# Raw keys and values summed by three adds on GpSimd and one reduction on VectorE, with the ranks' matmuls a tile later

## The chip, the cores and the metric

One core of a Trainium2 chip runs the whole program. The metric is the device time of one execution in microseconds. The kernel before took 1160.65 us, the median of three runs (1155.35 to 1163.43).

## What is computed

Eight batches of eight heads with 576 queries of 64 numbers go through an attention whose keys and values are first averaged over eight neighbours, so that 72 pooled keys per head are left. The 4608 rows of 512 numbers that result go through two mixtures of eight experts, one after the other; each row is sent to the expert with its largest gate logit.

```python
def _attn_ref(q, k, v):
    k_p = k.reshape(B, H, Sp, pool, D).mean(axis=3)
    v_p = v.reshape(B, H, Sp, pool, D).mean(axis=3)
    scores = scale * np.matmul(q, k_p.transpose(0, 1, 3, 2))
    scores = scores - np.max(scores, axis=-1, keepdims=True)
    attn = np.exp(scores)
    attn = attn / (np.sum(attn, axis=-1, keepdims=True) + 1e-09)
    return np.matmul(attn, v_p).astype(np.float32)

def _moe_ref(x, w_gate, w_output_gate, w1, w2):
    logits = x @ w_gate
    e_idx = np.argmax(logits, axis=1)
    ...
    for e in range(E):
        mask = e_idx == e
        h = np.maximum(x[mask] @ w1[e], 0.0)
        ye = h @ w2[e]
        out[mask] = gate_w[mask, None] * eom[mask, e, None] * ye
```

The second mixture has the same form, with a bias by modality in its logits and without the output gate.

## The kernel before

The program has two parts: an attention stage, and then the two layers of experts. The change edits the first.

**Tiles.** The 4608 queries are worked off in 36 tiles of 128 (`NT`), four and a half tiles to a batch. The loop at L639 runs over the tiles as a pipeline that is written out by hand: in turn i, TensorE computes the scores of tile i (L364), multiplies the transposed exponentials of tile i-2 with the values (L401) and transposes the exponentials of tile i-1 (L385). VectorE takes the maxima of tile i (L369) and normalises tile i-2 (L415 to L422). ScalarE takes the exponentials of tile i (L376) and evicts the transposes (L392). The order on each engine is the order of the code, and each engine takes its instructions in that order.

**Sums of raw keys and values.** Per batch, the eight planes of raw keys (and likewise of values) come in two loads of four planes into two tiles of a ring of seven (`ring`, L488). `pool_sum` (L298) adds them up: `half` adds planes 2 and 3 to planes 0 and 1 of one tile (L301, 576 elements per partition, on GpSimd), twice per sum; `both` on VectorE adds the two tiles (L305, 576 elements), gives the second tile back to the ring and adds the two planes that are left (L307, 288 elements); `spread` (L319 on ScalarE) copies the heads apart into KB, which the scores read, or VT, from which TensorE makes the values' operand VB (L332, L334). There are 16 such sums; the first keys are summed in another way (L526 to L531), and of the first values one half is added on VectorE, so that 15 sums have L305 and L307. The halves are handed out by `gp_work` at the end of a turn (two per turn, with scatters between them), and `both` and `spread` come three turns after the last half (`DELAY`), or earlier where a tile needs them.

**Routing.** The tiles form groups of four (`groups`, L347; two groups of two at the end). When a group's last tile is normalised, `route` (L427) puts a list of small operations for the whole group into `fill`: the choice of the expert (L451 to L458; L457 writes the one-hot of the choice in bf16), the ranks of the rows within their expert (`ranks`, L442: five small matmuls on TensorE, L445 and L447, that read that one-hot), the gate's factors (L460 to L463, L467, L469, L471, L472), the rows' places (L464 to L470), and last the hand-over of the group's scatters (L480, indirect DMAs on GpSimd) to the queue `gpq`. `filler` takes one entry at a time from the head of this list, about eight per turn, between VectorE's other work (two at a time while more than 16 are left). An entry with the letter "p" is TensorE's: `filler` at other places stops before it, and `filler(9, "p")` at the end of a turn, behind the transposes, takes it.

After the fourth group twelve more operations choose the favourite expert (L128 to L139), whose weights are then loaded in the attention stage and split into a high and a low part, one tile of weights per turn: the high part on ScalarE (L613, L616), the low one on GpSimd (L617).

**Layers.** Each expert's rows come back in blocks of 256; TensorE multiplies with three products of high and low parts (L757 and L799). The blocks' tiles xH and xL and the activations HH and HL lie in the pool `wp` behind the weights W1H and W1L (L100 to L107).

Of the kernel before, what the change touches and what calls it, by code (L numbers as in the profile page):

```python
# [10 lines left out]
F32R = mybir.dt.float32r  # L11
# [3 lines left out]
ALU = mybir.AluOpType  # L15
# [7 lines left out]
P = 128  # L23
# [10 lines left out]
NF = F // P  # L34
# [13 lines left out]
def kernel(ctx, tc, q, k, v, wg, wo, w1, w2, mod, wg2, bias2, v1, v2, out):  # L48
# [51 lines left out]
    W1H = [wp.tile([P, F], F32R, name=f"W1H{i}") for i in range(ND)]  # L100
    W1L = [wp.tile([P, F], F32R, name=f"W1L{i}") for i in range(ND)]
    W2H, W2L = [], []
    xH = wp.tile([P, ND, BLK], F32R, name="xH")
    xL = wp.tile([P, ND, BLK], F32R, name="xL")
    xg0 = wp.tile([P, 2, XW], F32, name="xg0")
    HH = [wp.tile([P, 2, BLK], F32R, name=f"hh{i}") for i in range(NF // 2)]
    HL = [wp.tile([P, 2, BLK], F32R, name=f"hl{i}") for i in range(NF // 2)]  # L107
    dummy = cst.tile([P, XW], F32, name="dummy")
    GP.memset(dummy, 0.0)
    GP.memset(dummy[:, DM + 1:DM + 2], float(N))  # L110
# [187 lines left out]
    def pool_sum(eng, first, raw, dst, scale):  # L298
        def half(lo, eng):
            r = raw[lo]  # L300
            eng.tensor_tensor(r[:, 0:2], r[:, 0:2], r[:, 2:4], op=ALU.add)  # L301

        def both():

            DVE.tensor_tensor(raw[0][:, 0:2], raw[0][:, 0:2], raw[4][:, 0:2], op=ALU.add)  # L305
            ring.append(raw[4])
            DVE.tensor_tensor(raw[0][:, 2], raw[0][:, 0], raw[0][:, 1], op=ALU.add)  # L307

        def spread():
            apart_heads(dst, raw[0][:, 2], slice(0, NG), scale)  # L310
            ring.append(raw[0])

        return [lambda: half(0, first), lambda: half(4, eng)], [both, spread]
# [34 lines left out]
    where = {T: (g, i) for g, ts in enumerate(groups) for i, T in enumerate(ts)}  # L348
    st, lgs, xgs, fill = {}, {}, {}, []

    def filler(n=1, kinds="v"):
        n += len(fill) > 16
        while n and fill and fill[0][0] in kinds:
            fill.pop(0)[1]()
            n -= 1
# [71 lines left out]
    def route(g):  # L427
        G = len(groups[g])
        T0 = groups[g][0]
        lg = lgs[g][:, 0:G, 0:E]  # L430
        og = lgs[g][:, 0:G, E:2 * E]
        bc = lambda t: t.unsqueeze(2).to_broadcast([P, G, E])
        c8 = lambda t: t.unsqueeze(1).to_broadcast([P, G, E])
        t5 = lambda n, dt=F32, bufs=2: sm.tile([P, 5], dt, name=n, bufs=bufs)[:, 0:G]
        t58 = lambda n, dt=F32: sm.tile([P, 5, E], dt, name=n)[:, 0:G]
        m, km, z, ez, df, ssum = (t5(n) for n in ("rm", "rkm", "rz", "rez", "rdf", "rss"))
        di = t5("rdi", I32, 3)
        a, oh, d, a2, ex, dd = (t58(n) for n in ("ra", "roh", "rd", "ra2", "rex", "rdd"))
        ohb = t58("rohb", BF16)
        pr = []  # L440

        def ranks():  # L442
            p = ranks_in[0]()
            pr.append(p)
            PE.matmul(p[:, 0:G], lhsT=tri_b, rhs=ohb, start=True, stop=False, skip_group_check=True)  # L445
            for dl in range(1, G + 1):
                PE.matmul(p[:, dl:G + 1], lhsT=ones_b, rhs=ohb[:, 0:G + 1 - dl], start=False, stop=dl == G, skip_group_check=True)  # L447

        V = lambda f: ("v", f)
        fill.extend([  # L450
            V(lambda: DVE.tensor_reduce(m, lg, axis=AX.X, op=ALU.max)),  # L451
            V(lambda: DVE.tensor_tensor(a, lg, bc(m), op=ALU.is_ge)),
            V(lambda: DVE.tensor_tensor(d, lg, bc(m), op=ALU.subtract)),
            V(lambda: DVE.tensor_tensor(a, a, c8(rev), op=ALU.mult)),
            V(lambda: ACT.activation(ex, d, AF.Exp)),
            V(lambda: DVE.tensor_reduce(km, a, axis=AX.X, op=ALU.max)),
            V(lambda: DVE.tensor_tensor(ohb, c8(rev), bc(km), op=ALU.is_equal)),  # L457
            V(lambda: DVE.tensor_tensor(oh, c8(rev), bc(km), op=ALU.is_equal)),  # L458
            ("p", ranks),
            V(lambda: DVE.tensor_tensor(a2, oh, og, op=ALU.mult)),  # L460
            V(lambda: DVE.tensor_reduce(ssum, ex, axis=AX.X, op=ALU.add)),
            V(lambda: DVE.tensor_reduce(z, a2, axis=AX.X, op=ALU.add)),
            V(lambda: ACT.activation(ez, z, AF.Exp, scale=-1.0)),  # L463
            V(lambda: DVE.tensor_tensor(dd, pr[0][:, 0:G], c8(base1), op=ALU.add)),  # L464
            V(lambda: DVE.tensor_tensor(base1, base1, pr[0][:, G], op=ALU.add)),
            V(lambda: DVE.tensor_tensor(dd, dd, oh, op=ALU.mult)),
            V(lambda: DVE.tensor_scalar(ssum, ssum, 1e-9, None, op0=ALU.add)),  # L467
            V(lambda: DVE.tensor_reduce(df, dd, axis=AX.X, op=ALU.add)),
            V(lambda: DVE.tensor_scalar(ez, ez, 1.0, None, op0=ALU.add)),  # L469
            V(lambda: DVE.tensor_copy(di, df)),  # L470
            V(lambda: DVE.tensor_tensor(ssum, ssum, ez, op=ALU.mult)),  # L471
            V(lambda: DVE.reciprocal(xgs[g][:, 0:G, DM], ssum)),  # L472
            V(lambda: gpq.extend((lambda i=i: scatter1(di, i, xgs[g])) for i in range(G))),
        ])
        if g == 3:
            fill.extend(V(f) for f in fav1)
            fill.append(V(lambda: sjobs.append(first_weights)))
# [159 lines left out]
            sjobs.append(load)  # L637

    for i in range(NT + 1):  # L639
        if 0 < i - 2 < NT:  # L640
            stage_et_evict(i - 2)
        if vbs:
            vbs.pop()()
        second = []
        if splits and (splits[0][0] <= i or i >= NT):
            first, *second = splits.pop(0)[1]
            first()
        if 0 < i < NT:
            for a in range(i == 2, 2):
                scores(i, a)  # L650
        if i == NT:
            t = turned(ps_a, ("ps0", "ps1"))
            turn(t, xg0, (0,))
        if 0 <= i - 2 < NT:
            stage_av(i - 2)
        if 0 < i < NT:
            for a in range(2):
                if i == 1:
                    v0.pop(0)()
                maxima(i, a)  # L660
                stage_exp(i, a)
        if i == 2:
            prefetch(2)
            load_q(2)
            flush(ldq, 2)
        if lasts and i >= summed.get(lasts[0][0], i) + DELAY:
            lasts.pop(0)[1]()
        filler()
        if 0 <= i - 2 < NT:
            normalise(i - 2)  # L670
        if 0 <= i - 1 < NT:
            stage_et(i - 1)
        if i == NT:
            stage_et_evict(i - 1)
            turn(t, xg0, (1,))
            high(t, xH)
            low(t, xH, xL)
            stage_av(i - 1)
            normalise(i - 1)
        else:  # L680
            filler(9, "p")
        filler()
        for _ in range(1 + i % 2):
            if ldq:
                ldq.pop(0)[1]()
        gp_work(2)
        if fetched == B - 1 and len(ring) == KV and not W2H and not ldq:
            kctx.close()
            w2p = ctx.enter_context(tc.tile_pool(name="w2p", bufs=1, side="right", reuse_waits="tile"))
            W2H += [w2p.tile([P, 2, DM], F32R, name=f"W2H{i}") for i in range(NF // 2)]  # L690
            W2L += [w2p.tile([P, 2, DM], F32R, name=f"W2L{i}") for i in range(NF // 2)]
        for f in second:
            f()
        if sjobs and len(splits) < 3 and (W2H or not late2[0]):
            f = sjobs.pop(0)()
            if isinstance(f, tuple):
                splits.append((i + 3, f))
        if i == 0:
            flush(sums, 1)
        if i == 1:  # L700
            v0.pop()()
            DVE.memset(KB[1], 0.0)
            DVE.memset(VT[1], 0.0)
            scores(2, 0)
            stage_et_evict(0)
            evicts = [prep_v(0, 0), prep_v(0, 1, "pm")]
            for f in evicts:
                f()
        if late:
            vbs.append(prep_v(*late.pop(0)))  # L710
        if i + 1 < NT:
            prepare(cols(i + 1)[-1][0], True)
        if i + 2 < NT:
            b = cols(i + 2)[-1][0]
            if b > prepped:
                prepare(b)
                prepped = b
                if 2 < b + 2 < B:
                    prefetch(b + 2)
        if i < NT and cols(i)[-1][0] > fetched - 2 and fetched + 1 < B:  # L720
            fetched += 1
            load_q(fetched)
        tags = {e[0] for e in sums}
        for tag in {e[0] for e in lasts} - tags - set(summed):
            summed[tag] = i
# [439 lines left out]
```

## Time and profile before

| | us |
|---|---|
| median of three runs | 1160.65 |
| the profiled execution | 1161.28 |
| its span, first to last instruction | 1159.6 |
| PE busy (share of the span) | 1081.8 (93%) |
| DVE busy | 661.0 (57%) |
| ACT busy | 395.0 (34%) |
| POOL busy | 271.0 (23%) |
| mean granted clock of TensorE | 0.973 |

All times in the rows further down are microseconds from the start of the span unless marked ns. PE is TensorE, DVE VectorE, ACT ScalarE, POOL GpSimd; L12 is line 12 of the kernel before. A busy PE counts matmuls that are pipelined, so its busy time is no measure of its peak; where it is idle, the bracket behind a row says for how long and what it waited for.

### The profile page before, as it was taken

The page shows a single profiled execution, that of the slowest core. Times are in us where ns is not written, and L with a number is a line of the kernel's source. Part 1 is how long each engine was busy: PE and PEld are TensorE (multiplying, and loading weights), DVE is VectorE, ACT ScalarE, POOL GpSimd, SP SyncE. Part 2 cuts the span into 40 slices and gives each one's busy share as a digit, 9 for nine tenths or more (in the row PEclk, how much of TensorE's full clock was granted, in tenths as well). Part 3 has the DMA queues.
Part 4 walks back from the last instruction along what each step waited for, and adds up shares of the span by engine and source line. Part 5 has one row for each costly group of instructions (what it writes and reads, how often), then busy time and mean ns, then how long its engine had stood idle before and what let it go on. Part 6 is the DMA issues. An engine that isn't in the chain of part 4 may idle for free. (4 is left out here: it accounts for less than half of the span.)

```text
span 1159.6 us, 21927 instructions
## 1 busy us (share of the span) xinstructions
PE 1081.8 (93%) x7058; PEld 970.4 (84%) x7058; DVE 661.0 (57%) x2154; ACT 395.0 (34%) x924; POOL 271.0 (23%) x249
## 2 busy tenths in 40 slices
PE   7988888999997999799999998999999999999993
PEld 6878787988876898688889977899889889988983
DVE  6988887777989877877987676111211221111110
ACT  6766674123634323314512232221212332211120
POOL 7545355100614400411610003100011040001000
PEclk8989998999999999899999998999999999999997
DMA  9766543641735511512450001721111111111000
GB/s 345 271 217 216 191 138 146 218 141 46 265 107 185 185 41 45 173 51 84 144 203 31 20 21 60 282 84 39 38 47 56 38 44 52 38 39 48 29 20 21
DMA packets 52090, 128.12 MB, mean 110 GB/s; under 512 B 6957, under 2 KB 10029, under 8 KB 51760
## 3 DMA queue, kind: packets, MB, share of 16 engines
q1 hardware_dynamic: 42928, 97.28, 25.5%
q0 software_dynamic: 8960, 28.47, 6.3%
q8 instruction: 88, 1.44, 0.5%
q14 instruction: 114, 0.93, 0.2%
HBM read 92.51 MB, written 34.27 MB: 109 GB/s over the span
## 5 line engine op out<-in xcount | busy, mean ns | idle before, releaser
L747 DVE SCALAR_TENSOR_TENSOR hl<-h,hh 128x512 fp32r<-128x512 f32 x140 | 94.9, 690 | 357.1 <-ACT hh L746 355.8
L799 PE MATMUL y<-W2H,hh 128*128 128x512 f32 x608 | 238.5, 403 | 11.4 <-DVEq L1024 8.0
L799 PE MATMUL y<-W2L,hh 128*128 128x512 f32 x608 | 238.2, 401 | 0.0
L799 PE MATMUL y<-W2H,hl 128*128 128x512 f32 x608 | 236.3, 400 | 1.2 <-DVE hl L747 1.1
L823 DVE CUSTOM_DVE_ANT_0 junk<-y,wg2b 128x512 f32<-128x512 f32 x312 | 192.9, 686 | 2.8 <-ACTq L1026 2.1
L746 ACT ACTIVATE hh<-h 128x512 fp32r<-128x512 f32 x140 | 83.4, 597 | 313.7 <-PE h L757 310.2
L802 ACT ACTIVATE y<-y,xg 128x512 f32<-128x512 f32 x76 | 52.3, 689 | 316.8 <-PE y L799 269.2
L799 PEld LDWEIGHTS y<-W2H,hh 128*128 128x128 f32 x608 | 115.6, 191 | 39.2 <-issue 7.1
L799 PEld LDWEIGHTS y<-W2H,hl 128*128 128x128 f32 x608 | 115.9, 191 | 31.1 <-DVE hl L747 3.5
L799 PEld LDWEIGHTS y<-W2L,hh 128*128 128x128 f32 x608 | 116.1, 191 | 25.8
L1046 POOL DMA_INDIRECT out_dram<-y,ti x37 | 36.4, 983 | 382.2 <-ACT y L802 259.0
L757 PE MATMUL h<-xH,W1L 128*128 128x256 f32 x608 | 123.5, 285 | 0.2 <-DVE W1L L193 0.2
L757 PE MATMUL h<-xH,W1H 128*128 128x256 f32 x608 | 99.9, 287 | 7.8 <-issue 3.8
L811 POOL TENSOR_TENSOR W2L<-R,W2H 128x1024 fp32r<-128x1024 f32 x32 | 76.9, 2435 | 121.3 <-ACT W2H L1028 101.7
L877 POOL DMA_INDIRECT xs<-y,qdi x39 | 38.5, 987 | 273.8 <-DVE lg L823 246.9
L757 PE MATMUL h<-x2H,W1L 128*128 128x256 f32 x512 | 102.2, 280 | 0.2 <-DVE W1L L193 0.2
L757 PE MATMUL h<-xL,W1H 128*128 128x256 f32 x608 | 98.2, 284 | 0.0
L757 PEld LDWEIGHTS h<-xH,W1L 128*128 128x128 f32 x608 | 95.5, 193 | 0.4 <-DVE W1L L193 0.4
L757 PEld LDWEIGHTS h<-xH,W1H 128*128 128x128 f32 x608 | 84.0, 193 | 8.4 <-issue 7.2
L757 PE MATMUL h<-x2H,W1H 128*128 128x256 f32 x512 | 82.7, 283 | 3.7 <-DVE qdd L867 3.3
L757 PEld LDWEIGHTS h<-xL,W1H 128*128 128x128 f32 x608 | 84.4, 193 | 0.0
L401 PE MATMUL pav<-VB,et 96*128 96x162 f32 (+1 forms) x480 | 72.8, 318 | 12.2 <-DVE ll L420 5.7
(245 smaller groups left out, 1646.5 us busy)
## 6 DMA issues: line engine op xcount, KB each, us to landing
R<-in_w_dram SPq DMA_DIRECT2D x56, 512.0 KB, 5.2
xg<-xs SPq DMA_DIRECT2D x72, 258.0 KB, 2.7
kv<-in_v_dram SPq DMA_DIRECT2D x16, 576.0 KB, 6.4
R<-in_v_dram SPq DMA_DIRECT2D x16, 512.0 KB, 7.5
kv<-in_k_dram SPq DMA_DIRECT2D x14, 576.0 KB, 5.2
qt<-in_q_dram SPq DMA_DIRECT2D x14, 576.0 KB, 9.5
xs<-dummy SPq DMA_DIRECT2D x18, 258.0 KB, 2.6
wraw<-in_w_dram SPq DMA_DIRECT2D x8, 512.0 KB, 3.9
```

Of the source, the lines that this page charges most:

```text
L401: PE.matmul(v4[r0:r0 + n, a, j:j + 2, :], lhsT=st[T]["et"][a][:, j, r0:r0 + n], rhs=VB[b % 3][:, a * 3 + j, :], start=j == 0, stop=j == 2, ...
L746: ACT.activation(HH[kk], p, AF.Relu)
L747: DVE.scalar_tensor_tensor(HL[kk], in0=p, scalar=0.0, in1=HH[kk].bitcast(F32), op0=ALU.max, op1=ALU.subtract)
L757: PE.matmul(p[:, c2, :], lhsT=W[d][:, c:c + P], rhs=x[:, d, :], start=n == 0, stop=n == 3 * ND - 1)
L799: PE.matmul(p, lhsT=X[f // 2][:, f % 2, hf * P:(hf + 1) * P], rhs=W[f // 2][:, f % 2, :], start=i == 0, stop=i == 3 * NF - 1)
L802: ACT.activation(S["y"][:, hf, 0:DM], p, AF.Copy, scale=S["xg"][:, hf, DM:DM + 1])
L811: GP.tensor_tensor(W2L[j], R2[j], W2H[j].bitcast(F32), op=ALU.subtract)
L823: DVE.tensor_tensor_reduce(out=M["junk"][:, e % 2], in0=p, in1=M["wg2b"][:, e, :], scale=1.0, scalar=0.0, op0=ALU.mult, op1=ALU.add, accum ...
L877: apart("xs2", GP.indirect_dma_start(xs2, IDX(ap=di[:, hf:hf + 1], axis=0), y[:, hf, :], None, bounds_check=E * REG - 1, oob_is_err=False))
L1046: apart("out", GP.indirect_dma_start(out, IDX(ap=S["ti"][:, hf:hf + 1], axis=0), S["y"][:, hf, 0:DM], None, bounds_check=N - 1, oob_is_err ...
```

## The change

`pool_sum` puts more of a sum on GpSimd. `half` writes its result into the first tile at once: the first half into planes 0 and 1, the second into planes 2 and 3 of the same tile. After the second half the second tile goes back to the ring, and a third add on the same engine adds planes 2 and 3 to planes 0 and 1. VectorE then sums the two planes that are left by one `tensor_reduce`, which reads them through a view with the plane innermost. For the first values, where VectorE does the second half, it does the third add too.

`route` marks the turn in which the one-hot is issued, and `filler(9, "p")` does nothing in that turn, so the ranks' matmuls are issued at the end of the next one at the earliest. The list is put into another order: the sum of the exponentials, its 1e-9 and the gate's exponential stand ahead of the ranks, and behind them stand nine entries instead of fourteen.

HH and HL are allocated right behind W1H and W1L, ahead of xH, xL and xg0.

```diff
     W2H, W2L = [], []
+    HH = [wp.tile([P, 2, BLK], F32R, name=f"hh{i}") for i in range(NF // 2)]
+    HL = [wp.tile([P, 2, BLK], F32R, name=f"hl{i}") for i in range(NF // 2)]
     xH = wp.tile([P, ND, BLK], F32R, name="xH")
     xL = wp.tile([P, ND, BLK], F32R, name="xL")
     xg0 = wp.tile([P, 2, XW], F32, name="xg0")
-    HH = [wp.tile([P, 2, BLK], F32R, name=f"hh{i}") for i in range(NF // 2)]
-    HL = [wp.tile([P, 2, BLK], F32R, name=f"hl{i}") for i in range(NF // 2)]
...
         def half(lo, eng):
             r = raw[lo]
-            eng.tensor_tensor(r[:, 0:2], r[:, 0:2], r[:, 2:4], op=ALU.add)
+            eng.tensor_tensor(raw[0][:, lo // 2:lo // 2 + 2], r[:, 0:2], r[:, 2:4], op=ALU.add)
+            if lo:
+                ring.append(r)
+                eng.tensor_tensor(raw[0][:, 0:2], raw[0][:, 0:2], raw[0][:, 2:4], op=ALU.add)
 
         def both():
 
-            DVE.tensor_tensor(raw[0][:, 0:2], raw[0][:, 0:2], raw[4][:, 0:2], op=ALU.add)
-            ring.append(raw[4])
-            DVE.tensor_tensor(raw[0][:, 2], raw[0][:, 0], raw[0][:, 1], op=ALU.add)
+            DVE.tensor_reduce(raw[0][:, 2], raw[0][:, 0:2].rearrange("p j c -> p c j"), axis=AX.X, op=ALU.add)
...
+    now, marked = [0], [0]
+
+    def mark():
+        marked[0] = now[0]
+
     def filler(n=1, kinds="v"):
+
+        if kinds == "p" and marked[0] == now[0]:
+            return
         n += len(fill) > 16
...
-            V(lambda: DVE.tensor_tensor(ohb, c8(rev), bc(km), op=ALU.is_equal)),
+            V(lambda: (mark(), DVE.tensor_tensor(ohb, c8(rev), bc(km), op=ALU.is_equal))),
             V(lambda: DVE.tensor_tensor(oh, c8(rev), bc(km), op=ALU.is_equal)),
-            ("p", ranks),
             V(lambda: DVE.tensor_tensor(a2, oh, og, op=ALU.mult)),
             V(lambda: DVE.tensor_reduce(ssum, ex, axis=AX.X, op=ALU.add)),
             V(lambda: DVE.tensor_reduce(z, a2, axis=AX.X, op=ALU.add)),
+            V(lambda: DVE.tensor_scalar(ssum, ssum, 1e-9, None, op0=ALU.add)),
             V(lambda: ACT.activation(ez, z, AF.Exp, scale=-1.0)),
+            ("p", ranks),
+            V(lambda: DVE.tensor_scalar(ez, ez, 1.0, None, op0=ALU.add)),
             V(lambda: DVE.tensor_tensor(dd, pr[0][:, 0:G], c8(base1), op=ALU.add)),
             V(lambda: DVE.tensor_tensor(base1, base1, pr[0][:, G], op=ALU.add)),
             V(lambda: DVE.tensor_tensor(dd, dd, oh, op=ALU.mult)),
-            V(lambda: DVE.tensor_scalar(ssum, ssum, 1e-9, None, op0=ALU.add)),
+            V(lambda: DVE.tensor_tensor(ssum, ssum, ez, op=ALU.mult)),
             V(lambda: DVE.tensor_reduce(df, dd, axis=AX.X, op=ALU.add)),
-            V(lambda: DVE.tensor_scalar(ez, ez, 1.0, None, op0=ALU.add)),
             V(lambda: DVE.tensor_copy(di, df)),
-            V(lambda: DVE.tensor_tensor(ssum, ssum, ez, op=ALU.mult)),
             V(lambda: DVE.reciprocal(xgs[g][:, 0:G, DM], ssum)),
...
     for i in range(NT + 1):
+        now[0] = i
```

Where the instructions stand, first on TensorE around the first group's ranks, in the kernel before: `ps` are scores, `pav` the values' products, `pe` the transposes, `rohb` the one-hot, `pm` the ranks.

```order
L385 MATMUL pe_660<-ident,ee 96x128 x3
L445 LDWEIGHTS tri_b
L445 MATMUL pm<-rohb,tri_b 128x32
L447 LDWEIGHTS ones_b
L447 MATMUL pm<-rohb,ones_b 128x32
...
L364 MATMUL ps_679<-KB_182,qt 128x144 x2
L364 MATMUL ps_682<-KB_182,qt 128x144 x2
L401 MATMUL pav<-VB_185,et_674 128x162 x3
```

And in the changed kernel, whose lines are some nine further down (L373 is the scores' line, L410 the values', L394 the transposes', L454 and L456 the ranks'):

```order
L394 MATMUL pe_665<-ident,ee 96x128 x3
L373 MATMUL ps_679<-KB_182,qt 128x144 x2
L373 MATMUL ps_682<-KB_182,qt 128x144 x2
L410 MATMUL pav<-VB_185,et_674 128x162 x3
L410 MATMUL pav<-VB_185,et_676 128x162 x3
L394 MATMUL pe_713<-ident,ee 96x128 x3
...
L454 LDWEIGHTS tri_b
L454 MATMUL pm<-rohb,tri_b 128x32
L456 LDWEIGHTS ones_b
L456 MATMUL pm<-rohb,ones_b 128x32
```

The ranks of a group have moved behind the next tile's scores, values' products and transposes.

Second, on GpSimd from one group's copy into its tile `x` to the next one's, in the kernel before: `kv` are tiles of the ring, `xs` takes the scatters.

```order
L411 COPY x<-meta 128x4x3
L301 TENSOR_TENSOR kv_196<-kv_196 128x576
L301 TENSOR_TENSOR kv_194<-kv_194 128x576
L480 DMA xs_66<-x,rdi 37888x516 x2
L301 TENSOR_TENSOR kv_198<-kv_198 128x576
L480 DMA xs_66<-x,rdi 37888x516
L301 TENSOR_TENSOR kv_197<-kv_197 128x576
L480 DMA xs_66<-x,rdi 37888x516
```

And in the changed kernel (L420 the copy, L301 a half, L304 the third add, L489 a scatter):

```order
L420 COPY x<-meta 128x4x3
L489 DMA xs_66<-x,rdi 37888x516 x2
L301 TENSOR_TENSOR kv_195<-kv_195 128x576
L301 TENSOR_TENSOR kv_195<-kv_197 128x576
L304 TENSOR_TENSOR kv_195<-kv_195 128x576
L301 TENSOR_TENSOR kv_194<-kv_194 128x576
L489 DMA xs_66<-x,rdi 37888x516
L301 TENSOR_TENSOR kv_194<-kv_199 128x576
L304 TENSOR_TENSOR kv_194<-kv_194 128x576
L489 DMA xs_66<-x,rdi 37888x516
```

Two of a group's four scatters have moved behind the next copy, and each sum has a third add right behind its second half.

Third, on VectorE the first tile's normalisation and the sum of the second batch's keys, in the kernel before:

```order
L305 TENSOR_TENSOR kv_198<-kv_198,kv_199 128x576
L307 TENSOR_TENSOR kv_198<-kv_198 128x288
L415 TENSOR_SCALAR rs<-pav 128x8
L417 RECIPROCAL rs<-rs 128x8
L419 TENSOR_TENSOR x<-pav,rs 128x512
L420 TENSOR_TENSOR ll<-pav,rs 128x128
L422 TENSOR_REDUCE lgs<-ll 128x16
```

And in the changed kernel (L424 to L431 the normalisation, L308 the reduction):

```order
L424 TENSOR_SCALAR rs<-pav 128x8
L426 RECIPROCAL rs<-rs 128x8
L428 TENSOR_TENSOR x<-pav,rs 128x512
L429 TENSOR_TENSOR ll<-pav,rs 128x128
L431 TENSOR_REDUCE lgs<-ll 128x16
L308 TENSOR_REDUCE kv_198<-kv_198 128x288
```

The sum has moved behind the normalisation.

## Rows read from the trace of the kernel before

**Rows 1.** Windows by stage: length, busy us of each engine, PEclk, DMA share, GB/s.

```profile
22.43:183.64 161.21, 134.33 (x1039) 125.58 (x1037) 139.49 (x404) 112.85 (x395) 83.29 (x69) 0.95 0.59 207
183.64:195.87 12.23, 11.27 (x69) 10.77 (x67) 7.74 (x34) 4.70 (x16) 1.73 (x2) 0.77 0.49 186
195.87:1159.60 963.73, 919.75 (x5842) 819.06 (x5841) 501.38 (x1694) 264.85 (x471) 167.95 (x124) 0.98 0.26 88
```

**Rows 2.** Waits of PE, 20 to 197 us: total us, times, longest us.

```profile
PE pm L445 <- DVE rohb L457: 14.6, 6, 4.5
PE pav L401 <- DVE ll L420: 5.7, 3, 3.3
```

**Rows 3.** Timeline of PE, DVE and POOL, 55 to 70 us: start, length, instruction, idle before.

```profile
56.38 0.82 PE L385 MATMUL pe<-ident,ee 128*96 128x128 f32 x6
59.75 0.19 PE L445 MATMUL pm<-rohb,tri_b 128*128 128x32 bf16 x1 [2.56 <-DVE rohb L457]
61.57 1.78 PE L364 MATMUL ps<-KB,qt 128*128 128x144 f32 x8
65.50 1.15 PE L364 MATMUL ps<-KB,qt 128*128 128x144 f32 x8
...
56.70 3.00 DVE L457 TENSOR_TENSOR rohb<-rev,rkm 128x32 bf16<-128x32 f32 x1
...
56.89 2.75 POOL L301 TENSOR_TENSOR kv<-kv 128x576 f32<-128x576 f32 x2
```

**Rows 4.** Six lines, 0 to 197 us: xcount, ns min/median/max, first and last start.

```profile
L457 DVE TENSOR_TENSOR rohb<-rev,rkm x9: 174/193/5429, 40.7 to 196.7; 128x32 bf16<-128x32 f32 x8, 128x16 bf16<-128x16 f32 x1
...
L305 DVE TENSOR_TENSOR kv<-kv,kv x15: 747/750/2896, 13.9 to 143.6; 128x576 f32<-128x576 f32 x15
...
L307 DVE TENSOR_TENSOR kv<-kv x15: 458/459/1872, 14.7 to 146.5; 128x288 f32<-128x288 f32 x15
...
L422 DVE TENSOR_REDUCE lgs<-ll x35: 354/368/376, 23.8 to 194.2; 128x16 f32<-128x128 f32 x35
...
L369 DVE TENSOR_REDUCE nm<-ps x72: 440/448/459, 8.4 to 185.9; 128x4 f32<-128x288 f32 x72
...
L301 POOL TENSOR_TENSOR kv<-kv x29: 1393/1408/1558, 11.2 to 135.0; 128x576 f32<-128x576 f32 x29
```

**Rows 5.** Timeline of DVE and POOL, 68 to 82 us.

```profile
68.77 0.13 DVE L472 RECIPROCAL x<-rss 128x4 f32<-128x4 f32 x1
77.61 3.01 DVE L457 TENSOR_TENSOR rohb<-rev,rkm 128x32 bf16<-128x32 f32 x1
...
69.69 1.01 POOL L480 DMA_INDIRECT xs<-x,rdi  x1 [10.05 <-DVE x L472]
77.81 2.75 POOL L301 TENSOR_TENSOR kv<-kv 128x576 f32<-128x576 f32 x2
```

**Rows 6.** Timeline of DVE and PE, 114 to 185 us.

```profile
114.66 2.90 DVE L136 CAST fei<-fef 128x2 int32<-128x2 f32 x1
...
178.02 5.43 DVE L457 TENSOR_TENSOR rohb<-rev,rkm 128x32 bf16<-128x32 f32 x1
...
120.29 3.02 PE L401 MATMUL pav<-VB,et 96*128 96x162 f32 x12 [3.31 <-DVE ll L420]
...
162.23 0.18 PE L445 MATMUL pm<-rohb,tri_b 128*128 128x32 bf16 x1 [1.85 <-DVE rohb L457]
...
183.50 0.18 PE L445 MATMUL pm<-rohb,tri_b 128*128 128x32 bf16 x1 [4.46 <-DVE rohb L457]
```

**Rows 7.** Timeline of ACT and PE, 20 to 26 us.

```profile
22.59 0.90 ACT L319 ACTIVATE KB<-kv 64x288 f32<-64x288 f32 x2 [0.36 <-DVE kv L307]
...
24.05 1.92 PE L401 MATMUL pav<-VB,et 96*128 96x162 f32 x12 [0.47 <-ACT et L392]
```

**Rows 8.** The page's costliest groups: first layer, the two x tiles.

```profile
L757 PE MATMUL h<-xH,W1L 128*128 128x256 f32 x608 | 123.5, 285 | 0.2 <-DVE W1L L193 0.2
L757 PE MATMUL h<-x2H,W1L 128*128 128x256 f32 x512 | 102.2, 280 | 0.2 <-DVE W1L L193 0.2
```

## The prediction

> **What bounds the kernel now.** I read the stretches first. From 195.87 us on, the two expert layers run with TensorE busy 919.8 of 963.7 us, and the change touches no instruction there. What it edits is in front: 33 starts of a tile's scores lie between 22.43 and 183.64 us, 161.2 us for 32 tiles, 5.04 us each, of which TensorE works 134.3 us at a granted clock of 0.95 [rows 1]. So the attention stage is where time can go, and a microsecond less there is a microsecond off the end, since the layers wait for the last tile.
>
> Next came the waits of TensorE in that stage. The largest is on the change's path: six times, 14.6 us in all, the ranks' matmuls (L445) wait for VectorE's one-hot (L457), and three times, 5.7 us, the values' matmuls (L401) wait for VectorE to empty their PSUM tile (L420) [rows 2]. TensorE takes its queue in order, so a wait of the ranks holds all behind it.
>
> Then I asked why VectorE is late, in the order of time around one such wait. The one-hot is an operation of 32 elements, and here it lasts 3.00 us: it starts at 56.70, GpSimd's two adds of raw values run from 56.89 to 59.64, and it ends just after them. TensorE is idle for 2.56 us, and the eight scores' matmuls behind it then take 1.78 us, where those of the next tile take 1.15 [rows 3]. The same operations elsewhere show the rule of this trace: the one-hot takes 0.174 to 5.429 us, the add of two SBUF planes (L305) 0.747 to 2.896, the next (L307) 0.458 to 1.872, while the reductions L422 and L369, one input each, stay within 0.354 to 0.376 and 0.440 to 0.459. GpSimd's add is hardly disturbed, 1.393 to 1.558 [rows 4]. So two-input work on VectorE pays for GpSimd's adds, and a request made just ahead of a run pays for the whole run.
>
> Last, why they meet in every group of four tiles. The scatters of a group wait on GpSimd for the group's last factor (L472, 68.77). The first starts at 69.69, and the queue that stood behind it is then worked off, down to two adds at 77.81 to 80.56, exactly when the next group's one-hot comes, at 77.61 (3.01 us) [rows 5].
>
> **The change part by part.**
>
> The sums. Per sum VectorE drops L305 and L307, 0.75 + 0.46 = 1.21 us undisturbed, and gets one reduction of 576 reads. No row shows that one; the contiguous reduction L369 gives 0.448 x 576/288 = 0.90 us, the strided L422 gives 0.368 x 576/128 = 1.66 us (fixed cost multiplied too). I take the middle, 1.28, because it steps between two planes for each result but writes few. Undisturbed VectorE gains nothing; it gains where the two adds were disturbed. It lies beside TensorE's work, so I book 0 by itself. GpSimd gets a third add of 1.41 us in 14 sums (the first values' stands on VectorE), 20 us, in a queue that mostly waits. The reduction now waits for the third add; behind it on VectorE stand a tile's maxima or its normalisation, for which ScalarE and then TensorE wait, and its cover is the distance of three tiles at which the code puts it (without that, 1.41 us per sum, the third rival).
>
> The order. The ranks now stand a tile later on TensorE, behind the next tile's scores, values and transposes, so the one-hot has a tile (5 us) to come. Nothing else is held: nobody reads the ranks before the fill list reaches them, and the list stops there for a tile. That stop is the second effect: the last factor comes at the end of its tile, the scatters are handed over a tile later, and on GpSimd the next keys' three adds stand behind two scatters. By the durations of rows 4 and 5, with the last factor at t: one scatter to t+1.3, two adds to t+4.1, three scatters to about t+8, three adds to t+12.3. The next group's selection (L452 to L458) falls at t+4 to t+6, beside scatters, and the three adds fall in the tile in which the list stands still. So the waits go, and do not only move.
>
> Gains: of the 14.6 us, 4.46 and 1.85 stand behind splits of weights on GpSimd [rows 6], which stay; the other four, 14.6 - 6.3 = 8.3, I count whole. Of the 6.3 I count half, 3.1: VectorE will be as late, but TensorE has a tile's work before it notices. The 5.7 us come with the choice of the favourite expert and an add: a cast of two numbers took 2.90 there, and the values' matmuls then waited 3.31 [rows 6]. One run of two adds still meets that list: half, 2.9. The clock: 134.3 x 0.05 = 6.7 us of TensorE's work is lost to the low level of 1.2 GHz, which the rows show behind such waits (3.02 us for twelve values' matmuls at 120.29 [rows 6], 1.92 for the twelve at 24.05 [rows 7]); half, 3.4. Together 17.7.
>
> Costs: the second batch's keys are now reduced behind tile 0's normalisation, so the copies into KB at 22.59, for which the evictions and then the values' matmuls at 24.05 wait [rows 7], come up to 2.3 us later; the next value sum, which met an add there, gives most of it back: 0.5, between 0 and 2.3. In the first group GpSimd has nine adds in a row, and the selection meets them: by the 3.00 us for two adds, three cost 4.4, less 1.6 paid there now: 2.8, between 0 and 4.4. By the Trainium skill (SBUF — State Buffer, Who interferes with whom) the loser is blocked until the first one's instruction ends, so a third add would cost nothing more and this term would be 0; rows 3 show a wait through two adds, so I keep the row's price. The first ranks of the layer get their one-hot some 0.4 us later, as four more operations stand ahead of it: 0.4, between 0 and 0.8.
>
> The activations' place: the same bytes at other addresses. The nearest rows are the two x tiles at different places, 285 and 280 ns per matmul [rows 8]; if 5 ns hung on the place, the 3 x 608 matmuls that read HH and HL would give or take 9 us. I take 0: the slower one also runs the first block, at the low clock.
>
> Sum: 17.7 - 0.5 - 2.8 - 0.4 = 14.0. The profiled execution took 1161.28 us, so 1147.3; it stands 0.6 above the median of the runs shown, so 1146.7, said as 1147.
>
> **The rivals.** First, the waits move: VectorE stays as late, and the values' matmuls wait in place of the ranks. For it: at 178.02 the one-hot takes 5.43, and pulled from TensorE's way it would still hold L420. Against it: the waits by adds depend on where the burst falls, and the burst moves. Then a fifth of 14.6 is left, 2.9 us: about 1158.
>
> Second, all goes: 14.6 + 5.7 + 6.7 = 27.0 less 0.9: about 1135. Against it: the splits of weights stay on GpSimd.
>
> Third, slower: the sums come onto the path. Each is then 1.41 + 1.28 - 1.21 = 1.48 us longer, 21 us over 14 sums, less the 8.3: about 1174. It decides where a sum ends after the place where the copies to KB or VT stand, three tiles behind the last add. For it: GpSimd's queue stands behind scatters for long stretches, as before 69.69, and the second batch's keys are that late already. Against it: three tiles are 15 us. The Trainium skill speaks for this rival (GPSIMD Engine Reference, Engine selection): elementwise work belongs on VectorE, GpSimd being about twice as slow with two inputs; rows 4 agree, 1.408 to 0.750.
>
> **How the numbers follow.** Forecast 0.42, waits move 0.30, all goes 0.17, slower 0.11. What a measurement of this kernel can tell from no change is about 1%, 11.6 us, so the border is 1149. The forecast's own range by its bounds is 1139 to 1154; 0.32 of it lies below the border, 0.10 above. Faster by over 1%: 0.32 + 0.17 + 0.02 of the first rival = 0.51. Slower: 0.11. Within: 0.38. The range reaches to the all-goes case and just past no change: 1132 to 1163.
>
> **What would show it.** In the new profile the ranks' matmuls wait for nothing; no wait of L401 on VectorE is above 2 us before 100 us; the one-hot of the first five groups is near 0.19 us; the new reduction lasts 0.9 to 1.7 us with hardly any spread; the granted clock between 22 us and the layers is 0.97 or more; the first layer's matmuls begin at about 182 instead of 195.87. It is wrong if the one-hot or L452 still shows waits of 3 to 4 us in most groups, if KB's copies wait for the reduction and the scores for KB, or if the layers' 963.7 us change.

## The result, and the profile after

| | before | after |
|---|---|---|
| median of nine runs, us | 1157.88 | 1148.03 |
| profiled execution / its span, us | 1161.28 / 1159.6 | 1147.13 / 1145.1 |
| first layer's matmuls begin, us | 195.87 | 184.41 |
| TensorE busy in the 32 tiles + from there to the layers, us | 134.33 + 11.27 | 136.11 + 9.29 |

The ratio is 0.9918, 95% interval [0.9892, 0.9944]: 9.9 us or 0.8% faster. The predicted 1147 is 1 us off, but part of that is luck: the three runs of before that were shown had a median of 1160.65, nine have 1157.88, so the forecast gain of 14.0 us was 9.9. And 0.8% lies within the 1% that was called no change, to which I had given 0.38, not above it, to which I had given 0.51.

Windows of the profile after, by stage, with the columns of [rows 1]:

```profile
23.32:173.92 150.60, 136.11 (x1034) 126.93 (x1032) 123.50 (x390) 110.88 (x389) 96.36 (x80) 0.94 0.61 215
173.92:184.41 10.49, 9.29 (x69) 8.42 (x70) 7.54 (x31) 6.64 (x23) 5.07 (x5) 1.00 0.71 266
184.41:1145.10 960.69, 917.02 (x5842) 819.95 (x5841) 500.23 (x1696) 265.09 (x472) 168.76 (x124) 0.98 0.26 89
```

The 32 tiles take 150.6 us where they took 161.2, the stretch behind them 10.5 where it took 12.2, and the layers begin 11.5 us earlier (the tiles themselves begin 0.9 us later). TensorE's granted clock is no better in the tiles, 0.94 for 0.95; in the stretch behind them it is 1.00 for 0.77. The layers are 3.0 us shorter; over the profiled executions of all kernels below they take 954.6 to 966.8 us, so that is no part of the change's effect that could be told apart.

What TensorE waits for, 16 to 200 us (total us, times, longest), to be held against [rows 2]:

```profile
PE pav L410 <- ACT et L401: 5.0, 6, 2.3
PE ps L373 <- DVE rs L424: 3.1, 2, 1.9
PE ps L373 <- ACT ee L385: 2.3, 6, 0.7
PE pav L410 <- DVE fef L135: 1.9, 1, 1.9
PE pav L410 <- DVE rz L470: 1.3, 1, 1.3
PE pv L333 <- ACT VT L320: 1.1, 1, 1.1
...
PE t L454 <- DVE rohb L466: 0.3, 1, 0.3
```

The 14.6 us of the ranks are gone: 0.3 us are left, in the last groups (tile `t`). New is a wait of the scores for a tile's first normalising operation (L424), 3.1 us at two places, and the scores' waits for ScalarE's exponentials (L385) rose from 0.9 us in one to 2.3 in six. The lines that answer to [rows 4] (count, ns min/median/max, first and last start):

```profile
L466 DVE TENSOR_TENSOR rohb<-rev,rkm x10: 175/192/886, 42.3 to 189.1; 128x32 bf16<-128x32 f32 x8, 128x16 bf16<-128x16 f32 x2
...
L308 DVE TENSOR_REDUCE kv<-kv x15: 746/753/773, 14.2 to 134.1; 128x288 f32<-128x576 f32 x15
...
L304 POOL TENSOR_TENSOR kv<-kv x14: 1398/1404/1413, 18.3 to 117.8; 128x576 f32<-128x576 f32 x14
...
L461 DVE TENSOR_TENSOR ra<-lgs,rm x10: 165/192/2935, 40.2 to 188.5; 128x32 f32<-128x32 f32 x8, 128x16 f32<-128x16 f32 x2
```

The one-hot's worst case fell from 5.429 to 0.886 us. The new reduction takes 0.753 with no spread at all. One steady group in order of time, DVE, POOL and PE (start, length, instruction, idle before), against [rows 3, 5]:

```profile
53.37 1.23 POOL L489 DMA_INDIRECT xs<-x,rdi  x1 [8.79 <-DVE x L481]
54.63 1.42 POOL L301 TENSOR_TENSOR kv<-kv 128x576 f32<-128x576 f32 x1
56.13 1.41 POOL L304 TENSOR_TENSOR kv<-kv 128x576 f32<-128x576 f32 x1
...
57.69 1.00 POOL L489 DMA_INDIRECT xs<-x,rdi  x1 [0.16 <-issue]
58.64 0.19 DVE L466 TENSOR_TENSOR rohb<-rev,rkm 128x32 bf16<-128x32 f32 x1
...
60.35 0.97 POOL L489 DMA_INDIRECT xs<-x,rdi  x1 [0.30 <-issue]
60.83 1.96 DVE L471 TENSOR_SCALAR rss<-rss 128x4 f32<-128x4 f32 x1
61.34 2.90 POOL L301 TENSOR_TENSOR kv<-kv 128x576 f32<-128x576 f32 x2
...
63.75 0.18 PE L454 MATMUL pm<-rohb,tri_b 128*128 128x32 bf16 x1
```

This is the forecast order: a scatter, two adds, three scatters with the selection beside them (the one-hot at 58.64 runs free), then the three adds of the next sum. What they block now (L471, 1.96 us) is a result that nobody waits for: the list stands still there, and the ranks at 63.75 start without a wait. It is not free, though. The tile's maxima stand behind it on VectorE and start at 62.70, and the scores behind the ranks wait 0.24 us for an exponential.

Two places went another way. The start, PE, ACT and DVE from 20 to 31 us, against [rows 7]:

```profile
24.50 0.75 DVE L308 TENSOR_REDUCE kv<-kv 128x288 f32<-128x576 f32 x1
...
25.29 0.90 ACT L320 ACTIVATE KB<-kv 64x288 f32<-64x288 f32 x2 [2.18 <-DVE kv L308]
...
26.75 3.05 PE L410 MATMUL pav<-VB,et 96*128 96x162 f32 x12 [2.29 <-ACT et L401]
29.59 1.40 PE L394 MATMUL pe<-ident,ee 128*96 128x128 f32 x6
```

The keys' copies start at 25.29 where they started at 22.59, and the values' matmuls behind them wait 2.29 us and then run 3.05 us where they took 1.92. And the weight splits, 147 to 153 us:

```profile
147.75 2.94 DVE L461 TENSOR_TENSOR ra<-lgs,rm 128x32 f32<-128x32 f32 x1
148.26 2.37 POOL L626 TENSOR_TENSOR W1L<-wraw,W1H 128x1024 fp32r<-128x1024 f32 x1
152.16 0.72 PE L373 MATMUL ps<-KB,qt 128*64 128x144 f32 x8 [1.86 <-DVE rs L424]
```

### The profile page after: what moved, and what is told of

The parts are those of the page before. It is cut to its first block, busy times and chain, and to the rows that moved or that the text cites. A ratio compares the mean times of both kernels' runs of the same rounds, so it can differ in the third digit from the quotient of the medians.

```text
span 1145.1 us, 21935 instructions
## 1 busy us (share of the span) xinstructions
PE 1079.9 (94%) x7058; PEld 971.3 (85%) x7058; DVE 642.7 (56%) x2140; ACT 395.2 (35%) x924; POOL 289.2 (25%) x263
## 5 line engine op out<-in xcount | busy, mean ns | idle before, releaser
L809 PE MATMUL y<-W2H,hh 128*128 128x512 f32 x608 | 236.1, 400 | 8.5 <-DVEq L1034 4.6
L809 PE MATMUL y<-W2L,hh 128*128 128x512 f32 x608 | 234.7, 396 | 0.0
L410 PE MATMUL pav<-VB,et 96*128 96x162 f32 (+1 forms) x480 | 73.4, 317 | 9.8 <-ACT et L401 5.0
```

Of the source, the lines that this page charges most:

```text
L410: PE.matmul(v4[r0:r0 + n, a, j:j + 2, :], lhsT=st[T]["et"][a][:, j, r0:r0 + n], rhs=VB[b % 3][:, a * 3 + j, :], start=j == 0, stop=j == 2, ...
L809: PE.matmul(p, lhsT=X[f // 2][:, f % 2, hf * P:(hf + 1) * P], rhs=W[f // 2][:, f % 2, :], start=i == 0, stop=i == 3 * NF - 1)
```

## The experiments

All ratios are to the kernel before, measured beside it; "layers at" is where the first layer's matmuls begin in the profiled execution.

| kernel | layers at, us | median, us | ratio, 95% |
|---|---|---|---|
| after | 184.41 | 1148.03 | 0.9918 [0.9892, 0.9944] |
| sums only | 192.14 | 1158.22 | 0.9988 [0.9964, 1.0011] |
| ranks and list only | 186.24 | 1147.69 | 0.9895 [0.9858, 0.9933] |
| place only | 196.04 | 1155.86 | 0.9977 [0.9949, 1.0006] |
| after, place put back | 182.99 | 1151.03 | 0.9914 [0.9882, 0.9946] |
| after, list held but ranks put back | 183.10 | 1148.07 | 0.9925 [0.9893, 0.9957] |
| after, early keys | 180.99 | 1144.77 | 0.9899 [0.9866, 0.9933] |
| after, four planes | 185.52 | 1150.61 | 0.9940 [0.9913, 0.9968] |
| after, splits on VectorE | 178.38 | 1142.18 | 0.9874 [0.9838, 0.9909] |
| after, both repairs | 175.26 | 1135.23 | 0.9798 [0.9759, 0.9836] |
| both repairs, place put back | 174.19 | 1137.59 | 0.9831 [0.9796, 0.9867] |
| both repairs, no adds beside the choice | 179.83 | 1138.02 | 0.9846 [0.9806, 0.9886] |
| before, ranks and splits | 177.71 | 1146.44 | 0.9903 [0.9868, 0.9939] |

**The three parts alone.** Each is the kernel before with one hunk of the diff: `pool_sum`; the list with `mark` and `now`; the two lines of HH and HL.

> The kernel before with the new sums alone. My theory: ranks stay ahead of the next tile's scores and still wait for the one-hot, now through runs of three adds; the immune reduction gives a little, the later first reduction takes 2 to 3 us: ratio 0.998 to 1.006, and TensorE still shows 10 us or more of waits of the ranks. Rival (the sums carry the gain, the ranks' place only shows it): ratio 0.990 to 0.995 and the ranks' wait under 6 us.

> The kernel before with the ranks a tile later and the new list alone. My theory: this part carries the gain, and without the late first reduction of the new sums it keeps 2 to 3 us more: ratio 0.987 to 0.992, ranks wait for nothing, first layer at 181 to 185 us. Rival (sums carry it): ratio 0.995 to 1.000, the waits moved to the values' matmuls behind VectorE's two-input adds.

> The kernel before with the activations next to W1 alone. My theory: other addresses, no change: ratio 0.998 to 1.002, layers 963 to 964 us in the profile. Rival (the 3 us that the layers took less in the changed kernel come from the addresses): ratio 0.996 to 0.998, layers about 961 us.

The sums alone change nothing that the medians show, and the ranks still wait 13.0 us. In the profiled execution their layers begin 3.7 us earlier than before; the interval, down to 0.9964 or 4.2 us, does not exclude that. The ranks with their list alone give the whole gain, though in the profiled execution their layers begin at 186.24, 1.8 us later than in the change and beyond the 181 to 185 expected. Each kernel has one profile: those that differ in the place alone begin their layers 0.2, 1.1 and 1.4 us apart, so differences of that size tell nothing. Waits of TensorE, 16 to 200 us, of the sums alone and then of the ranks alone:

```profile
PE pm L446 <- DVE rohb L458: 13.0, 5, 4.5
```

```profile
PE pav L409 <- ACT et L400: 6.0, 9, 1.0
PE pav L409 <- DVE fef L135: 4.3, 1, 4.3
PE ps L372 <- DVE rs L423: 3.1, 2, 1.9
```

In the second the ranks wait 0.3 us as in the change, the longest wait on a copy is 1.0 where the change has 2.3 at the start, and the choice of the favourite expert costs 4.3 in place of 1.9. So by these rows the sums take 2.4 us from one wait and add 1.3 to another; no gain of theirs on top of the ranks shows in the medians.

**The place put back.** The two lines of HH and HL back where they were, in the changed kernel and, with the last run, in the best one:

> The changed kernel with the activations' place put back. My theory: the same as the changed kernel, ratio 0.990 to 0.994, layers within 2 us of 960.7. Rival (addresses give the layers' 3 us): ratio 0.994 to 0.996, layers about 963.7 us.

> The kernel with both repairs, the activations' place put back to that of the kernel before: a second look at the place, and at how well the gain of both repairs stands. My theory: the place does nothing: ratio 0.977 to 0.986, layers begin at 174 to 177 us. Rival (the place gives part of the gain): 0.987 to 0.990 with the same start of the layers.

0.9914 against 0.9918 with the new place, and 0.9831 against 0.9798; alone 0.9977 with 1 inside its interval. Two of these three comparisons favour the new place and one the old, each by less than its intervals: the place alone is worth no more than 0.5%, the lower end of its interval, and whether it is worth anything stays open. The place alone came out just outside what was expected (0.998 to 1.002), in the range of its rival, and its layers take 959.3 us in the profiled execution where they took 963.7; the place put back, with 962.7, lies between the two.

**List held, ranks put back.** An empty entry "h" holds the list for a tile, as the ranks do in the change; the ranks' entry stands behind the one-hots again.

```
-        if kinds == "p" and marked[0] == now[0]:
+        if kinds == "h" and marked[0] == now[0]:
...
             V(lambda: DVE.tensor_tensor(oh, c8(rev), bc(km), op=ALU.is_equal)),
+            ("p", ranks),
...
             V(lambda: ACT.activation(ez, z, AF.Exp, scale=-1.0)),
-            ("p", ranks),
+            ("h", lambda: None),
...
+            filler(9, "h")
             filler(9, "p")
```

> The changed kernel with the ranks' matmuls put back a tile earlier, behind the one-hot's own tile, while the list stands still for a tile as in the change: VectorE's and GpSimd's orders stay, only TensorE's differs. My theory of the prediction, that the adds are moved away from the selection: the one-hot stays under 1 us, the ranks wait under 3 us in all outside the two splits of weights, ratio 0.990 to 0.995. Rival (only the tile of slack on TensorE counts): the ranks wait 8 to 14 us again, ratio 0.997 to 1.002.

PE, the ranks' first matmul in five of the eight groups of four:

```profile
57.21 0.18 PE L454 MATMUL pm<-rohb,tri_b 128*128 128x32 bf16 x1
...
74.82 0.18 PE L454 MATMUL pm<-rohb,tri_b 128*128 128x32 bf16 x1
...
113.49 0.18 PE L454 MATMUL pm<-rohb,tri_b 128*128 128x32 bf16 x1 [1.98 <-DVE rohb L466]
...
151.06 0.18 PE L454 MATMUL pm<-rohb,tri_b 128*128 128x32 bf16 x1 [1.72 <-DVE rohb L466]
...
172.45 0.18 PE L454 MATMUL pm<-rohb,tri_b 128*128 128x32 bf16 x1 [1.11 <-DVE rohb L466]
```

With the ranks back in their old place on TensorE, the second, third and fourth group, which waited 2.56, 3.57 and 1.45 us before, wait for nothing: moving the adds away from the selection did that, not the tile of slack. The slack is needed only beside the choice and the splits, 4.8 us in three waits, where the change has 3.1 + 1.3 in other waits (L424, L470) instead. So the two kernels take the same time.

**Early keys.** `lasts.pop(0)[1]()` in the third tile, ahead of `prefetch(2)`: the reduction of the second batch's keys goes back in front of tile 0's normalisation, where the ring's shortage of buffers had forced it before.

> The changed kernel with the reduction of the second batch's keys put back in front of tile 0's normalisation. My theory: the change's late reduction holds KB's copies, then the evictions and the values' matmuls at 26.75 (2.3 us), and the low clock behind them costs more; here these go, the third tile starts near 27.5 instead of 30.9, the layers 2 to 4 us earlier: ratio 0.988 to 0.991. Rival (the start catches up by itself, the next tiles wait for values and transfers anyway): 0.991 to 0.993, the layers begin at 184 as in the change.

```profile
20.36 0.75 DVE L308 TENSOR_REDUCE kv<-kv 128x288 f32<-128x576 f32 x1
...
21.72 0.91 ACT L320 ACTIVATE KB<-kv 64x288 f32<-64x288 f32 x2
...
23.19 1.92 PE L410 MATMUL pav<-VB,et 96*128 96x162 f32 x12
24.95 0.82 PE L394 MATMUL pe<-ident,ee 128*96 128x128 f32 x6
```

That is the timeline of the start with the reduction 4.1 us earlier: no wait, 1.92 + 0.82 us where the change took 3.05 + 1.40, and the layers begin 3.4 us earlier. By the rows it is 1.8 us of wait (2.29 in the change, 0.47 before) and 1.7 of low clock, 3.5. In the medians (1144.77 to 1148.03) it is as much, though the two intervals overlap. What the late start had hidden shows up behind it: the first group's wait for L470 is 1.89 us here (at 41.61) and 1.31 in the change.

**Four planes.** No third add: VectorE reduces four planes into the buffer that the second half came from.

```
-                ring.append(r)
-                eng.tensor_tensor(raw[0][:, 0:2], raw[0][:, 0:2], raw[0][:, 2:4], op=ALU.add)
...
-            DVE.tensor_reduce(raw[0][:, 2], raw[0][:, 0:2].rearrange(...)
+            DVE.tensor_reduce(raw[4][:, 0], raw[0].rearrange(...)
+            ring.append(raw[0])
```

> The changed kernel without the third add: VectorE reduces all four planes, 1152 reads; the ring then forces the keys' early reduction too. My theory: a one-input reduction runs at its rate beside GpSimd's adds, 1.4 to 1.6 us each, 10 us more of VectorE in idle time, and runs of two adds in place of three block less: ratio 0.986 to 0.990, like the early reduction alone or 1 to 2 us better, the first group's selection blocked at most 3 us. Rival (VectorE's queue is the bound, each 0.7 us is paid): 0.992 to 0.998.

```profile
L305 DVE TENSOR_REDUCE kv<-kv x15: 2133/2177/2210, 14.0 to 135.3; 128x288 f32<-128x1152 f32 x15
```

A miss: twice the reads take 2.9 times as long, 2.177 us against 0.753. It too has hardly any spread beside the adds. With 1.4 us more of VectorE in each of 14 sums the layers begin at 185.52, later than in the change and 4.5 us later than with early keys, although the start is repaired here too (0.78 us of wait for 2.29). So the third add on GpSimd is worth its 1.4 us.

**Splits on VectorE.** The eight low parts of the first weights are subtracted by VectorE: in `halves`, `GP.tensor_tensor(lo, ...)` becomes `DVE.tensor_tensor(lo, ...)`.

> The changed kernel with the eight low parts of the first weights subtracted on VectorE in place of GpSimd. My theory: the selection at 147.75 and 169.93, blocked 2.9 and 2.5 us by a split, runs free, the scores' waits at 152.16 and 173.92 (3.1 us) and the low clock behind them go; VectorE pays 8 x 1.33 = 10.6 us in a stretch where it idles: ratio 0.987 to 0.991. Rival (VectorE's work of 1.33 us falls on the same places): 0.992 to 0.997, TensorE waits there as long.

```profile
146.50 0.19 DVE L461 TENSOR_TENSOR ra<-lgs,rm 128x32 f32<-128x32 f32 x1
146.61 1.22 DVE L626 TENSOR_TENSOR W1L<-wraw,W1H 128x1024 fp32r<-128x1024 f32 x1
```

The operation that was blocked for 2.94 us takes 0.19, the scores' waits for L424 are gone from the list of waits (those of the values' matmuls for L470 rise from 1.3 to 3.3 us), and a split costs VectorE 1.22 us where GpSimd took 2.37. The layers begin 6.0 us earlier.

**Both repairs, and one too many.**

> The changed kernel with both repairs: the second batch's keys reduced early, the weights' low parts on VectorE. My theory: the two gains stand in different places and add, 3.4 us at the start and 6.0 at the splits: the layers begin at 174 to 176 us, ratio 0.983 to 0.987. Rival (the second is hidden by what the first uncovers): no better than the splits alone, 0.987 to 0.989, layers at 178.

> The kernel with both repairs, and GpSimd hands out no add of a sum while the list chooses the favourite expert. My theory: that choice runs beside adds at 102 to 112 us and its tile takes 9.9 us where others take 4.4; without adds beside it 3 to 5 us go: layers 3 to 5 us earlier than with both repairs, ratio 0.979 to 0.984. Rival (the nine adds then come in a row and meet the next group's selection, or the sums come late for the copies): within 1 us of both repairs, or later.

The two gains add: 184.41 - 3.4 - 6.0 = 175.0, and the layers begin at 175.26. This is the best kernel, 2.0% below the kernel before; the ratio is better than the 0.983 to 0.987 expected, though 0.983 still lies within its interval. The window of its tiles, as above:

```profile
22.47:165.49 143.02, 131.92 (x1037) 123.26 (x1035) 122.81 (x400) 111.24 (x393) 83.05 (x76) 0.98 0.67 234
```

Here the granted clock of the tiles rises, 0.98 for 0.94, and TensorE's busy time falls, 131.9 for 136.1.

Holding GpSimd's adds back while the favourite is chosen (a flag in `gp_work`) is the rival's case. DVE, POOL and PE of that kernel, 101 to 116 us:

```profile
101.66 0.26 DVE L130 SCALAR_TENSOR_TENSOR ft<-fn,fm,rev 128x8 f32<-128x8 f32 x1
102.95 0.26 DVE L132 TENSOR_SCALAR feh<-rev,fm 128x8 f32<-128x8 f32 x1
...
112.79 2.88 POOL L301 TENSOR_TENSOR kv<-kv 128x576 f32<-128x576 f32 x2
...
113.14 1.10 DVE L467 TENSOR_TENSOR rohb<-rev,rkm 128x32 bf16<-128x32 f32 x1
...
115.18 3.58 PE L411 MATMUL pav<-VB,et 96*128 96x162 f32 x12 [3.06 <-DVE ll L430]
```

The first half of the choice runs free, 0.26 us where the change had 0.83 and 1.58, but the wait for the choice (L135) is 1.89 us, as with both repairs alone (1.85): GpSimd, which runs ahead, starts the nine held adds at 104.13, beside the second half of the choice (L139 takes 1.38 us). They come in a row and meet the next selection too: its values' matmuls wait 3.06 us and then run at the low level, 3.58 us for twelve. So a choice wholly without adds beside it was not measured. The layers begin 4.6 us later than with both repairs, 1.2 us of which stand at the start already.

**The old sums with ranks and splits.**

> The kernel before with the ranks a tile later and the weights' low parts on VectorE, the sums as before. My theory: the new sums are worth little beside these; ratio 0.982 to 0.987, within 3 us of the kernel with both repairs. Rival (the immune reduction is what the list needs once the ranks are later): 0.988 to 0.992.

The layers begin 2.5 us later than with both repairs, as much as the wait for the choice is longer here (4.3 us for 1.9). The medians differ by 11 us, and the ratio lies in the rival's range, so the sums may be worth more in this company than the stage shows. Where the rest of the 11 us lies is in no profile: the execution profiled here was the fastest of its six, that of both repairs the slowest. It stays unexplained.

## Why the prediction was right, and which terms were not

The mechanism held. What was late were VectorE's small operations beside GpSimd's adds; the adds meet them less once the scatters are handed over a tile later; and it is that move, more than the ranks' new place, which frees the steady groups (list held, ranks put back).

- **Ranks, 8.3 + 3.1 us.** Right in size and place. The ranks' 14.6 us are gone and 3.1 us came back as the scores' waits at the two splits: 11.5 us net for 11.4. That a tile's work would cover half of the splits' waits was right too (6.3 to 3.1).
- **The values' matmuls, 2.9 us.** Right in kind, a little low: of the 5.7 us of waits on VectorE beside the choice and the add, 1.9 are left, a gain of 3.8 us.
- **The clock, 3.4 us.** It did not come where it was booked: in the tiles TensorE is busy 136.1 us for 134.3, at 0.94 for 0.95, and in the stretch behind them 9.3 for 11.3. That is 0.2 us net. Of the loss 1.7 us are new, at the start (next point), so 1.9 came elsewhere, about half of the term. Waits that stay or are new still have the low level behind them: twelve values' matmuls take 3.05 us behind 2.29 us of wait (26.75), 3.58 behind 1.86 (109.82) and 3.61 at 153.99, where they take 1.92 at the high level. Not every wait does: behind the 1.31 us at 45.81 they take 1.89. I took half of the waits for half of the loss, without asking where the waits that stay would stand.
- **The start, 0.5 us (0 to 2.3).** The step that was mis-sized most: 3.4 us, by the early keys. The copies into KB came 2.7 us later (0.9 of it stands ahead of the tiles), above the bound; nothing gave it back, and behind the wait the low level cost 4.45 - 2.74 = 1.7 us more, which the bound left out.
- **The first group, 2.8 us (0 to 4.4).** Less than priced: the selection meets the adds, and the values' matmuls then wait 1.3 us for it. From the scores at 39.45 to those at 56.34 the group takes 16.9 us, before from 36.00 to 53.43 it took 17.4. DVE, POOL and PE, 42 to 48 us:

```profile
42.32 0.89 DVE L466 TENSOR_TENSOR rohb<-rev,rkm 128x32 bf16<-128x32 f32 x1
...
43.11 1.47 POOL L301 TENSOR_TENSOR kv<-kv 128x576 f32<-128x576 f32 x1
...
43.34 1.29 DVE L468 TENSOR_TENSOR ra<-roh,lgs 128x32 f32<-128x32 f32 x1
...
45.81 1.89 PE L410 MATMUL pav<-VB,et 96*128 96x162 f32 x12 [1.31 <-DVE rz L470]
```

  I had priced three adds in a row at three adds' wait. Here the operation at 43.34 ends with the one add that it stands beside, and in the whole change no operation waits longer than 2.94 us; the one at 60.83 ends with the first of the two adds behind it, while in [rows 3] it was both. By the Trainium skill (SBUF — State Buffer, Who interferes with whom) a blocked VectorE instruction waits for the whole of the one ahead of it, and by that rule the term would have been 0, where 1.3 was paid. The operations at 43.34 and 60.83 agree with the rule; the two adds of [rows 3] are more than it gives. With early keys alone, and with both repairs, the group's wait is 1.89 us; behind it came the high level in the first kernel and the low one in the second:

```profile
41.61 1.89 PE L410 MATMUL pav<-VB,et 96*128 96x162 f32 x12 [1.89 <-DVE rz L470]
```

```profile
41.88 3.37 PE L410 MATMUL pav<-VB,et 96*128 96x162 f32 x12 [1.89 <-DVE rz L470]
```

- **The layer's first ranks, 0.4 us.** They wait 0.3.
- **The reduction.** It was booked at 0 in the sum and is not late anywhere but at the start. Its duration, 0.753 us, lies below my bounds of 0.90 to 1.66: both had scaled a duration with the reads, though in [rows 4] 128 reads take 0.368 us and 288 take 0.448. That the adds do not touch it is as predicted from [rows 4]. The Trainium skill (SBUF — State Buffer, Who interferes with whom) says that this instruction never contends with GpSimd on this chip; 746 to 773 ns in 15 cases agrees.
- **The place of HH and HL, 0.** Not refuted, within 0.5%.
- **The range.** The 1139 to 1154 called the forecast's own do not follow from the bounds given: those of the costs alone leave gains of 10.2 to 17.7 us, 1143 to 1150, and for the gains none are given.

These terms give 11.5 + 3.8 + 1.9 - 3.4 - 1.3 - 0.3 = 12.2 us, where 14.0 was forecast and the layers began 11.5 us earlier; 0.7 us lies in short waits that I did not take apart, among them the scores' for the exponentials. The mis-sized terms partly made up for each other: the start cost 2.9 us more and the clock gave 1.5 less, while the first group cost 1.5 less and the values' matmuls gave 0.9 more. That the medians differ by 9.9 us and not 11.5 is within what the layers vary by.

Of the rivals, "the waits move" came true at the splits, 3.1 of the 14.6 us, and with 1.3 in the first group. "The sums come onto the path" fell: the third add of one sum ends at 74.02 and its reduction starts at 87.51, 13.5 us of cover for a price of 1.4; the cover was short only for the second batch, whose values' third add ended at 24.02, 1.9 us before its reduction. "All goes", 1135 us, is not what the change does, but the two repairs reach it: they remove the late start and the splits' waits, two of the things for which the forecast had kept something back.

```profile
72.62 1.40 POOL L304 TENSOR_TENSOR kv<-kv 128x576 f32<-128x576 f32 x1
...
87.51 0.75 DVE L308 TENSOR_REDUCE kv<-kv 128x288 f32<-128x576 f32 x1
```

Of what was to show it, the ranks, the waits before 100 us and the reduction's lack of spread came; the one-hot is 0.19 us in four of the first five groups (0.89 in the first); the clock (0.95 from 22 us to the layers, 0.94 before, not 0.97) and the start of the layers (184.4, not 182) did not.

## What to carry to other kernels

When small operations of VectorE are held up by GpSimd, first ask whether the two can be made to fall at different times: handing GpSimd's other work over a tile later freed the selections of three groups, for scores' waits of a few tenths of a microsecond. An edit that frees a buffer earlier also takes away whatever that shortage forced to happen early; look for what moves back. And price the low clock behind a wait of TensorE at the place where a wait stays, as a cost that may come or not, and not as a share of all waits.

## What the runs showed of the hardware

- A reduction over strided planes takes 0.753 us for two planes (576 reads) and 2.177 us for four (1152 reads), with the same 288 results: 1.31 and 1.89 ns per read. Why the larger one is slower per read was not tried.
- An operation with one input in SBUF can be blocked too: the addition of a constant to four numbers took 1.96 us (L471 at 60.83), where it takes 0.16 with GpSimd idle (at 45.98); none of the reductions was. The Trainium skill (SBUF — State Buffer, Who interferes with whom) counts such scalar operations among those that may contend; the trace agrees.
- A subtraction of 1024 columns takes VectorE 1.22 us and GpSimd 2.37, so an engine that is "free" was holding the other for longer than the other would have needed for the work (2.94 us at 147.75).
- After a wait of 1.89 us at the same place in two kernels TensorE ran twelve matmuls in 1.89 us in one and in 3.37 in the other (41.61 and 41.88 above): the granted clock behind a wait is not the same each time.
